# Reordering seven products and two copies in an attention and expert kernel

## The chip, the cores and the metric

The kernel runs on one core of a Trainium2 chip. The metric is the device time of one execution in microseconds (us); the time of a kernel is the median of several runs. "The profiled execution" is one further run, recorded by the hardware profiler; all rows below are from it.

## The reference

Block-sparse attention (4 batches, 8 heads, 768 tokens, head size 64) feeds a layer of four experts, all in float32:

```python
def _moe_ref(x, domain_probs, w1, w2):          # x: 3072 x 512
    p = domain_probs / (domain_probs.sum(-1, keepdims=True) + 1e-09)
    out = np.zeros((N, D), dtype=np.float32)
    for e in range(E):                           # E = 4
        h = np.maximum(x @ w1[e], 0.0)           # 512 -> 1024
        out += p[:, e:e + 1] * (h @ w2[e])       # 1024 -> 512
    return out
```

Every token passes through all four experts; `x` is the attention output, 768 tokens a batch.

## The kernel before

**Work.** The 4 x 1024 hidden features are cut into 8 chunks of 512. In batches two to four (`b` = 1 to 3 in the code) each chunk has a first layer (`first7`, 512 inputs to 512 features) and a second layer (`second7`, back to 512 outputs). Both use a seven-product scheme of Strassen's kind, with the products numbered 1 to 7: one product is six matmuls of 128x128 weights by 384 tokens (two parts of the inner dimension, three combinations of high and low halves of the float32 numbers). In the first layer a chunk has two halves, `s` = 0 and 1, of seven products each, so 14 in all; the second layer has 14 as well (`SEQ`: seven products by two parts `d`). Chunk 0 of a batch is an exception: its first layer is done plainly (`FIRST7`), as 16 products, because the operands of the scheme are only being made then.

**Accumulators.** The first layer's products 1, 6, 7 and 4 are added up in one PSUM tile, `w`, one after another: W = P1, then P1+P6, then +P7, then +P4. After each but the last the running sum is read out by another engine, and the next of them may write only when that read is done. Products 2, 5 and 3 go to a tile `v`, of which there are two buffers; the second layer uses `v` too, and tiles `u0`, `u1` of its own. There is one buffer of `w`, so product 1 of the next half has to wait until the last reader of the half before it is through.

**Evacuation.** The 384-token results of a half are combined in tiles `ha` (named by `block(g, half)` in the code). `finish` (L889) takes ReLU and multiplies by the expert's weight of each token: one VectorE instruction, which reads either PSUM (`ha<-v,pb`, `ha<-w,pb`) or, for the two blocks that were already combined in SBUF, SBUF (`ha<-ha,pb`). The other sums are VectorE additions (L912, L916, L919, L922), and two copies are on ScalarE (L910, L914).

**From first to second layer.** `hidden` makes the second layer's operands from the finished `ha` tiles: sums and differences, and for each operand a ScalarE cast to the high half (L934) and a GpSimd subtraction for the low half (L935). Each second-layer product is added by VectorE to the running outputs `tot` (L1021), once or twice; product 5 goes to two outputs. In chunk 0 the first of these are ScalarE copies (L1019).

**What sets the order.** All engines run the program's order; there is no reordering scheduler. `experts` writes it: it emits first-layer and second-layer products alternately, the second layer of one chunk beside the first layer of the next, so that a second-layer product stands between two first-layer ones, except for two places in each batch, since chunk 0 has two more products. While batches two and three are in this stage, attention work of the next batch is put in between at given times (`drive`). Weights come by DMA in the products' order (`operands`, L674), and the conversion of the next batch's inputs is tied to positions in the list of products. The last chunk of the last batch has its own order (`SEQ_END`, `STEPS_END`) and ends with four stores of 384 KB.

Of the kernel before, what the change touches and what calls it, by code (L numbers as in the profile page):

```python
# [17 lines left out]
P = 128  # L18
# [5 lines left out]
def attention_moe_kernel(ctx: ExitStack, tc, qb, kb, vr, sampled, sampled_t, probs, w1, w2, out):  # L24
# [556 lines left out]
    def convert(b, limit=PLAIN):  # L581
        if b in pieces and steps.get(b, 0) < limit:
# [4 lines left out]
    L = len(ORDER)  # L587

    FIRST = [((0, 0, 0), 0), ((0, 1, 0), 0), ((1, 0, 0), 0), ((0, 0, 1), 2), ((0, 1, 1), 2),
             ((1, 1, 0), 0), ((1, 0, 1), 2), ((1, 1, 1), 2)]  # L590
# [49 lines left out]
    def operands():  # L640
# [29 lines left out]
        for b in range(1, B):  # L670
            for c in range(NCH):
                for s, n in ORDER if c else PLAIN8:
                    o = wp.tile([P, 2, KH, P], F32R, name="wo", bufs=NWO)
                    nc.sync.dma_start(f32(o), kept1[c, s, n])  # L674
                    wo[b, c, s, n] = o
                    yield
# [201 lines left out]
    def first7(b, c, s, n):  # L878
# [26 lines left out]
        else:  # L905
            if n == 1:
                W[s] = ps_m.tile([P, HS], F32, name="w", bufs=1)
            product(W[s], w, x, n == 1)
        if n == 2:
            nc.scalar.copy(block(0, 0), v)  # L910
        elif n == 1:
            nc.vector.tensor_add(block(0, 0), W[s], block(0, 0))  # L912
        elif n == 5:
            nc.scalar.copy(block(1, 1), v)  # L914
        elif n == 6:
            nc.vector.tensor_add(block(1, 0), W[s], block(1, 1))  # L916
            finish(0, 0, block(0, 0))
        elif n == 3:
            nc.vector.tensor_add(v, v, block(1, 0))  # L919
            finish(0, 1, v)  # L920
        elif n == 7:
            nc.vector.tensor_add(block(1, 1), W[s], block(1, 1))  # L922
        else:
            finish(1, 0, W[s])
            finish(1, 1, block(1, 1))
        next(weights, None)
# [3 lines left out]
    def hidden(b, c):  # L930
# [13 lines left out]
        if last_one(b, c):  # L944
# [11 lines left out]
            two(6, a11)  # L956
            nc.vector.tensor_sub(a12, a12, a11)
            yield
# [34 lines left out]
    def second7(b, c, i):  # L993
# [20 lines left out]
        for g, dh in (TO_END if last else TO)[n]:  # L1014
# [5 lines left out]
            else:  # L1020
                nc.vector.tensor_add(t, ps, t)  # L1021
            if c == NCH - 1 and (LAST_END if last else LAST)[g, dh] == n and d:
                nc.sync.dma_start(bass.AP(out.tensor, out.offset + b * S * DM + dh * (DM // 2) * S + g * HS,
                                          [[S, P], [P * S, 2], [1, HS]]), tot.pop((g, dh)))
        if d:
# [9 lines left out]
    def experts():  # L1035
# [48 lines left out]
        for b in range(1, B):  # L1084
            for c in range(NCH):
                one += ([(b, c, s, n) for s, n in ORDER] if c else
                        [(b, 0, s, (half, k, g)) for s, half, g in FIRST7 for k in range(2)])
# [272 lines left out]
```

## Time and profile before

| | |
|---|---|
| median of 3 runs | 1231.64 us (1229.37 to 1233.04) |
| profiled execution | 1228.22 us, span 1226.4 us |
| TensorE matmul busy | 1188.4 us (97%) |
| VectorE busy | 809.3 us (66%) |
| GpSimd busy | 838.6 us (68%) |
| ScalarE busy | 520.6 us (42%) |
| first layer, batches two to four, chunks 1 to 7 | 42 halves of seven products |
| steady chunk of batch four | 29.1 us, 28 products |

A row of the timeline gives the start and the length in us, the engine, the line, the operation, output and inputs, their shapes, how many instructions are merged, and in brackets how long the engine had been idle and what it waited for. A row of waits gives who waited for whom, the total in us, how often, and the longest. PE is TensorE, PEld its weight loads, DVE VectorE, ACT ScalarE, POOL GpSimd, SPq the DMA queue of SyncE. A TensorE row of six matmuls lasts 1.20 us from the first start to the modelled end, but the next product starts 1.04 us after it.

### The profile page before, as it was taken

Reading aid. Unit: us, or ns where it says so; the run is one execution under the profiler, and the core shown is the slowest. Engines: PE = TensorE matmul, PEld = TensorE weight load, DVE = VectorE, ACT = ScalarE, POOL = GpSimd, SP = SyncE. Lnnn points to the kernel's source line nnn. Section 1 sums busy time; section 2 is a strip of 40 time slices with the busy share of each in tenths; the row PEclk is TensorE's granted clock in tenths of the full one; section 3 lists DMA queues with packets and bytes.
Section 4 is the critical chain, followed back from the end, with each engine's and each line's share of the span. In section 5 each row is a group of like instructions: output and inputs, shape, how many; then the busy total and the mean of one; then the engine's idle time right before and its main releaser. Section 6 shows DMA issues by size and latency. Waiting matters only on the chain.

```text
span 1226.4 us, 32022 instructions
## 1 busy us (share of the span) xinstructions
PE 1188.4 (97%) x12243; PEld 1094.1 (89%) x12243; DVE 809.3 (66%) x1701; ACT 520.6 (42%) x1259; POOL 838.6 (68%) x824
## 2 busy tenths in 40 slices
PE   7789999999999999999999999999999999999997
PEld 4578888888888988989989998999999999999997
DVE  6675766566654767667666766766566676666667
ACT  4754565656552344445433243444533332222221
POOL 7737978888776675677647875766755776666662
PEclk9989999999999999999999999999999999999999
DMA  9986879999879887889969687889876688777774
GB/s 271 253 279 239 302 254 353 298 317 328 291 264 345 285 244 228 270 269 274 277 205 346 218 270 230 281 272 277 281 243 212 221 271 270 248 263 256 256 236 154
DMA packets 206804, 326.48 MB, mean 266 GB/s; under 512 B 17483, under 2 KB 108204, under 8 KB 206652
## 3 DMA queue, kind: packets, MB, share of 16 engines
q1 hardware_dynamic: 200208, 303.53, 75.9%
q0 software_dynamic: 6400, 20.91, 5.7%
q8 instruction: 97, 1.59, 0.6%
q14 instruction: 55, 0.45, 0.1%
q10 hardware_dynamic: 44, 0.00, 0.0%
HBM read 256.69 MB, written 67.68 MB: 264 GB/s over the span
## 4 chain that ended last, share of the span: by engine, by line
PE 76%; DVE 4%; DMA 3%; issue 2%; POOL 1%; ACT 1%; SPq 0%; DVEq 0%; ACTq 0%; POOLq 0%
PE w L770 18%; PE u L1011 15%; PE v L770 14%; PE v L1011 12%; PE po L848 7%; PE o L403 3%; PE tp L390 2%; PE s L369 2%; PE s L362 1%; DMA kept<-w2o 1%; DMA w2o<-kept 1%; PE x L422 1%; DMA v<-in_vr_dram 1%; PE sw L440 1%; DVE tot L1021 1%
## 5 line engine op out<-in xcount | busy, mean ns | idle before, releaser
L935 POOL TENSOR_TENSOR ho<-ha,ho 128x768 fp32r<-128x768 f32 x165 | 318.7, 1941 | 244.1 <-ACT ho L934 241.2
L770 PE MATMUL w<-xo,wo 128*128 128x384 f32 x1524 | 308.9, 339 | 6.8 <-DVE ha L922 3.2
L770 PEld LDWEIGHTS w<-xo,wo 128*128 128x128 f32 x1524 | 267.6, 188 | 14.7 <-DVE ha L922 3.9
L934 ACT CAST ho<-ha 128x768 fp32r<-128x768 f32 x168 | 139.3, 837 | 270.0 <-DVE ha L889 106.0
L770 PE MATMUL v<-xo,wo 128*128 128x384 f32 x1176 | 239.6, 340 | 2.4 <-DMA wo<-kept 1.1
L1011 PE MATMUL u<-ho,w2o 128*128 128x384 f32 x1128 | 228.2, 338 | 2.3 <-issue 2.3
L770 PEld LDWEIGHTS v<-xo,wo 128*128 128x128 f32 x1176 | 207.4, 189 | 7.9 <-DMA wo<-kept 1.4
L1011 PEld LDWEIGHTS u<-ho,w2o 128*128 128x128 f32 x1128 | 196.9, 188 | 4.7 <-issue 2.9
L1011 PE MATMUL v<-ho,w2o 128*128 128x384 f32 x888 | 179.6, 339 | 2.8 <-issue 1.5
L1011 PEld LDWEIGHTS v<-ho,w2o 128*128 128x128 f32 x888 | 154.7, 188 | 6.5 <-DVE ha L889 2.7
L1021 DVE TENSOR_TENSOR tot<-v,tot 128x384 f32<-128x384 f32 x184 | 97.9, 552 | 91.3 <-PE v L1011 89.9
L1021 DVE TENSOR_TENSOR tot<-u,tot 128x384 f32<-128x384 f32 x180 | 98.8, 552 | 47.2 <-PE u L1011 47.1
L848 PE MATMUL po<-w2o,hh 128*128 128x512 f32 x384 | 123.5, 403 | 1.9 <-DVE oacc L863 1.9
L381 ACT ACTIVATE p<-p,mx 128x256 f32<-128x256 f32 (+1 forms) x192 | 95.3, 498 | 52.4 <-DVE mx L379 52.3
L220 POOL DMA_INDIRECT v<-in_vr_dram,vidx x81 | 79.8, 985 | 23.7 <-issue 17.2
L660 POOL TENSOR_TENSOR wo<-r,wo 128x256 fp32r<-128x256 f32 x92 | 72.5, 793 | 32.2 <-ACT wo L659 31.6
L379 DVE CUSTOM_DVE_ANT_1 p<-s,mask 128x256 f32<-128x256 f32 (+1 forms) x192 | 69.7, 418 | 21.3 <-PE s L369 16.8
L889 DVE SCALAR_TENSOR_TENSOR ha<-ha,pb 128x384 f32<-128x384 f32 x84 | 83.1, 989 | 0.0
L848 PEld LDWEIGHTS po<-w2o,hh 128*128 128x128 f32 x384 | 69.0, 188 | 12.6 <-DVE oacc L863 2.7
L848 PE MATMUL po<-w2o,hl 128*128 128x512 f32 x192 | 75.8, 395 | 0.0
L403 PEld LDWEIGHTS o<-v,pt 128*32 128x32 f32 x2816 | 46.4, 110 | 21.6 <-issue 17.7
L403 PE MATMUL o<-v,pt 128*32 128x64 f32 x2816 | 55.2, 221 | 7.7 <-issue 7.0
(169 smaller groups left out, 1628.2 us busy)
## 6 DMA issues: line engine op xcount, KB each, us to landing
w2o<-kept SPq DMA_DIRECT2D x168, 512.0 KB, 4.7
wo<-kept SPq DMA_DIRECT2D x318, 256.0 KB, 4.1
kept<-wo SPq DMA_DIRECT2D x106, 256.0 KB, 5.0
v<-in_vr_dram SPq DMA_DIRECT2D x88, 192.0 KB, 6.3
kept<-w2o SPq DMA_DIRECT2D x32, 512.0 KB, 5.4
r<-in_w_dram SPq DMA_DIRECT2D x16, 512.0 KB, 5.5
r<-in_w_dram SPq DMA_DIRECT2D x32, 256.0 KB, 5.4
kept<-t SPq DMA_DIRECT2D x32, 256.0 KB, 5.9
```

The lines of the kernel that those rows point to most:

```text
L220: nc.gpsimd.indirect_dma_start(out=v[:rows, i, 1 - i], out_offset=None, in_=vr, element_offset=b * S * DM, in_offset=bass.IndirectOffsetOn ...
L379: nc.vector.tensor_tensor_reduce(p.rearrange("p (a b) -> p a b", b=BLOCK), s[h][:n, i], mk, -SCALE, 3.0e38, ALU.add, ALU.min, mx[:n])
L381: nc.scalar.activation(p, p, AF.Exp, bias=mx[:n], scale=-1.0, accum_out=self.sums[:n, m:m + 1])
L403: nc.tensor.matmul(o[cs, m], self.pt[:, 2 * m + k, cs], vs[c][:, k, e], start=k == 0, stop=k == 1)
L660: nc.gpsimd.tensor_sub(o[:, 1], src, f32(o[:, 0]))
L770: nc.tensor.matmul(ps, w[:, wi, t], x[:, xi, t], start=fresh and m == 0, stop=m == 3 * KH - 1, skip_group_check=not fresh)
L848: nc.tensor.matmul(p, a[:, js], w[:, i], start=f == 0 and n == 0, stop=f == FT - 1 and n == 2)
L889: nc.vector.scalar_tensor_tensor(block(g, half), src, 0.0, q, op0=ALU.max, op1=ALU.mult)
L934: nc.scalar.copy(o[:, 0], src)
L935: eng.tensor_sub(o[:, 1], src, f32(o[:, 0]))
L1011: nc.tensor.matmul(ps, w[:, j, wi, ds], h[:, hi, j], start=fresh and m == 0, stop=m == 5, skip_group_check=not fresh)
L1021: nc.vector.tensor_add(t, ps, t)
```

## The change

In chunks 1 to 7 of batches two to four the first layer's products come in the order 1 2 6 5 7 3 4 in place of 2 1 5 6 3 7 4. The sums are formed another way: ScalarE copies W after product 1 and after product 6, and `v` after product 5; VectorE adds `v` of products 2 and 5 to them, and W of product 7 to the copy of 5. The finish of block (1, 1), which followed product 4, now follows product 3. In the last chunk the difference a12 - a11 is computed on GpSimd instead of VectorE, and the last output block is stored in two DMAs of 192 KB, each as soon as its part is done, instead of one of 384 KB.

```diff
@@ -586,6 +586,9 @@
     ORDER = [(s, n) for s in range(2) for n in (2, 1, 5, 6, 3, 7, 4)]
     L = len(ORDER)
+    ORDER7 = [(s, n) for s in range(2) for n in (1, 2, 6, 5, 7, 3, 4)]
@@ -669,7 +672,7 @@
-                for s, n in ORDER if c else PLAIN8:
+                for s, n in ORDER7 if c else PLAIN8:
                     o = wp.tile([P, 2, KH, P], F32R, name="wo", bufs=NWO)
                     nc.sync.dma_start(f32(o), kept1[c, s, n])
@@ -906,23 +909,24 @@
             product(W[s], w, x, n == 1)
-        if n == 2:
-            nc.scalar.copy(block(0, 0), v)
-        elif n == 1:
-            nc.vector.tensor_add(block(0, 0), W[s], block(0, 0))
+        if n == 1:
+            nc.scalar.copy(block(0, 0), W[s])
+        elif n == 2:
+            nc.vector.tensor_add(block(0, 0), v, block(0, 0))
+        elif n == 6:
+            nc.scalar.copy(block(1, 0), W[s])
+            finish(0, 0, block(0, 0))
         elif n == 5:
             nc.scalar.copy(block(1, 1), v)
-        elif n == 6:
-            nc.vector.tensor_add(block(1, 0), W[s], block(1, 1))
-            finish(0, 0, block(0, 0))
+            nc.vector.tensor_add(block(1, 0), v, block(1, 0))
+        elif n == 7:
+            nc.vector.tensor_add(block(1, 1), W[s], block(1, 1))
         elif n == 3:
             nc.vector.tensor_add(v, v, block(1, 0))
             finish(0, 1, v)
-        elif n == 7:
-            nc.vector.tensor_add(block(1, 1), W[s], block(1, 1))
+            finish(1, 1, block(1, 1))
         else:
             finish(1, 0, W[s])
-            finish(1, 1, block(1, 1))
         next(weights, None)
@@ -954,7 +958,7 @@
             two(6, a11)
-            nc.vector.tensor_sub(a12, a12, a11)
+            nc.gpsimd.tensor_sub(a12, a12, a11)
@@ -1019,9 +1023,12 @@
-            if c == NCH - 1 and (LAST_END if last else LAST)[g, dh] == n and d:
-                nc.sync.dma_start(bass.AP(out.tensor, out.offset + b * S * DM + dh * (DM // 2) * S + g * HS,
-                                          [[S, P], [P * S, 2], [1, HS]]), tot.pop((g, dh)))
+            if c == NCH - 1 and (LAST_END if last else LAST)[g, dh] == n:
+                at0 = out.offset + b * S * DM + dh * (DM // 2) * S + g * HS
+                if last and n == 3:
+                    nc.sync.dma_start(bass.AP(out.tensor, at0 + d * P * S, [[S, P], [1, HS]]), t)
+                elif d:
+                    nc.sync.dma_start(bass.AP(out.tensor, at0, [[S, P], [P * S, 2], [1, HS]]), tot.pop((g, dh)))
@@ -1083,7 +1090,7 @@
-                one += ([(b, c, s, n) for s, n in ORDER] if c else
+                one += ([(b, c, s, n) for s, n in ORDER7] if c else
```

Three places show what it does to the engines' order. The first is TensorE in a steady chunk of batch four, from product 7 or 3 of half 0 to the first products of half 1. L770 (now L773) is a first-layer product, whose number follows `xo`; L1011 (now L1015) is a second-layer product. Before:

```order
L770 MATMUL v_15508<-xo3_14220,wo_15367 128x384 x6
L1011 MATMUL v_15519<-ho_15410,w2o_15377 128x384 x6
L770 MATMUL w_15447<-xo7_14557,wo_15386 128x384 x6
L1011 MATMUL v_15541<-ho_15414,w2o_15395 128x384 x6
L770 MATMUL w_15447<-xo4_14462,wo_15405 128x384 x6
L1011 MATMUL u0_15458<-ho_15444,w2o_15442 128x384 x6
L770 MATMUL v_15567<-xo2_14112,wo_15433 128x384 x6
L1011 MATMUL v_15578<-ho_15414,w2o_15395 128x384 x6
L770 MATMUL w_15592<-xo1_14137,wo_15455 128x384 x6
```

And now:

```order
L773 MATMUL w_15458<-xo7_14585,wo_15399 128x384 x6
L1015 MATMUL v_15552<-ho_15444,w2o_15409 128x384 x6
L773 MATMUL v_15565<-xo3_14248,wo_15421 128x384 x6
L1015 MATMUL v_15577<-ho_15448,w2o_15430 128x384 x6
L773 MATMUL w_15458<-xo4_14490,wo_15439 128x384 x6
L1015 MATMUL u0_15492<-ho_15478,w2o_15476 128x384 x6
L773 MATMUL w_15602<-xo1_14164,wo_15467 128x384 x6
L1015 MATMUL v_15613<-ho_15448,w2o_15430 128x384 x6
```

Between 7 and 4, which share a `w`, there were one product and there are now three; between 4 and the next half's product 1, which uses the same buffer, there were three and there is now one.

The second place is VectorE over the same products: additions (L919, L922; now L925, L923), finishes (L889, now L892) and the second layer's additions to `tot` (L1021, now L1025). Before:

```order
L919 TENSOR_TENSOR v_15508<-v_15508,ha_15473 128x384
L889 SCALAR_TENSOR_TENSOR ha_15473<-v_15508,pb_14820 128x384
L1021 TENSOR_TENSOR tot_14581<-v_15519,tot_14581 128x384
L922 TENSOR_TENSOR ha_15473<-w_15447,ha_15473 128x384
L1021 TENSOR_TENSOR tot_14665<-v_15541,tot_14665 128x384
L1021 TENSOR_TENSOR tot_14667<-v_15541,tot_14667 128x384
L889 SCALAR_TENSOR_TENSOR ha_15431<-w_15447,pb_14820 128x384
L889 SCALAR_TENSOR_TENSOR ha_15473<-ha_15473,pb_14820 128x384
```

And now:

```order
L923 TENSOR_TENSOR ha_15506<-w_15458,ha_15506 128x384
L1025 TENSOR_TENSOR tot_14609<-v_15552,tot_14609 128x384
L925 TENSOR_TENSOR v_15565<-v_15565,ha_15506 128x384
L892 SCALAR_TENSOR_TENSOR ha_15506<-v_15565,pb_14850 128x384
L892 SCALAR_TENSOR_TENSOR ha_15506<-ha_15506,pb_14850 128x384
L1025 TENSOR_TENSOR tot_14695<-v_15577,tot_14695 128x384
L1025 TENSOR_TENSOR tot_14697<-v_15577,tot_14697 128x384
L892 SCALAR_TENSOR_TENSOR ha_15465<-w_15458,pb_14850 128x384
```

The finish that reads SBUF only (`ha<-ha`) stood behind the one that releases `w` (`ha<-w`); it now stands ahead of it, with the two additions to `tot`.

The third place is TensorE where a batch goes from chunk 0 to chunk 1, the last two products of chunk 0 and the first of chunk 1. Before:

```order
L770 MATMUL w_14510<-xo7_14198,wo_14217 128x384 x6
L1011 MATMUL u1_14301<-ho_14394,w2o_14392 128x384 x6
L770 MATMUL w_14510<-xo3_14220,wo_14361 128x384 x6
L770 MATMUL v_14546<-xo2_14112,wo_14378 128x384 x6
L770 MATMUL w_14562<-xo1_14137,wo_14404 128x384 x6
```

And now:

```order
L773 MATMUL w_14538<-xo7_14227,wo_14245 128x384 x6
L1015 MATMUL u1_14329<-ho_14422,w2o_14420 128x384 x6
L773 MATMUL w_14538<-xo3_14248,wo_14389 128x384 x6
L773 MATMUL w_14574<-xo1_14164,wo_14406 128x384 x6
L773 MATMUL v_14590<-xo2_14139,wo_14432 128x384 x6
```

Product 1, which writes `w`, now follows the last product of chunk 0, which writes `w` as well, with nothing between them.

## The prediction

> **What bounds the kernel now.** I read the page first, then TensorE's waits, then the stretches, then the timeline of one steady chunk.
>
> ```profile
> PE 1188.4 (97%) x12243; PEld 1094.1 (89%) x12243; DVE 809.3 (66%) x1701; ACT 520.6 (42%) x1259; POOL 838.6 (68%) x824
> PEclk9989999999999999999999999999999999999999
> PE 76%; DVE 4%; DMA 3%; issue 2%; POOL 1%; ACT 1%; SPq 0%; DVEq 0%; ACTq 0%; POOLq 0%
> ```
>
> TensorE is the bound, at a granted clock of 0.8 in one slice of forty and 0.9 or more in the others. The change removes no product, so it can only shorten or lengthen the time in which TensorE stands still. In batch four there is none of that to take:
>
> ```profile
> 1000.00:1200.00 200.00, 200.00 (x1156) 199.98 (x1155) 132.66 (x219) 55.44 (x86) 132.06 (x70) 1.00 0.77 252
> ```
>
> Matmul busy is 200.00 of 200.00 us (second number). The waits on the results that the change rearranges all lie before that, in batches two and three:
>
> ```profile
> PE w L770 <- DVE ha L922: 3.2, 2, 1.6
> PE w L770 <- DVE ha L912: 1.3, 1, 1.3
> PE v L1011 <- DVE ha L889: 0.9, 2, 0.6
> ```
>
> These three, 5.4 us, are all that a better order can win here. The first is product 4 held by the addition that reads W after product 7, which is the tightest spot of the old order.
>
> **The change part by part.** Four accumulating products share one `w`. The new order moves the tight spot from 7→4 to 4→next 1. Whether that costs anything is read from a steady chunk of batch four; in this stretch the first-layer products of half 0 are 3, 7, 4 and then product 2 of half 1:
>
> ```profile
> 1095.05 0.57 DVE L919 TENSOR_TENSOR v<-v,ha 128x384 f32<-128x384 f32 x1 [0.29 <-PE v L770]
> 1095.65 0.56 DVE L889 SCALAR_TENSOR_TENSOR ha<-v,pb 128x384 f32<-128x384 f32 x1
> 1095.89 1.20 PE L770 MATMUL w<-xo,wo 128*128 128x384 f32 x6
> 1096.93 1.20 PE L1011 MATMUL v<-ho,w2o 128*128 128x384 f32 x6
> 1096.95 3.65 POOL L935 TENSOR_TENSOR ho<-ha,ho 128x768 fp32r<-128x768 f32 x2 [0.94 <-ACT ho L934]
> 1097.13 0.56 DVE L922 TENSOR_TENSOR ha<-w,ha 128x384 f32<-128x384 f32 x1 [0.46 <-PE w L770]
> 1097.97 1.20 PE L770 MATMUL w<-xo,wo 128*128 128x384 f32 x6
> 1098.17 1.02 DVE L1021 TENSOR_TENSOR tot<-v,tot 128x384 f32<-128x384 f32 x2 [0.48 <-PE v L1011]
> 1099.21 0.56 DVE L889 SCALAR_TENSOR_TENSOR ha<-w,pb 128x384 f32<-128x384 f32 x1
> 1099.69 1.33 DVE L889 SCALAR_TENSOR_TENSOR ha<-ha,pb 128x384 f32<-128x384 f32 x1
> 1100.05 1.20 PE L770 MATMUL v<-xo,wo 128*128 128x384 f32 x6
> 1100.95 0.54 DVE L1021 TENSOR_TENSOR tot<-u,tot 128x384 f32<-128x384 f32 x1
> ```
>
> A product's result can be read 1.24 us after its start (1095.89 to 1097.13). A dependent VectorE instruction follows 0.60 us after the one ahead of it (1095.05, 1095.65), an independent one 0.48 (1099.21, 1099.69). The last row of `finish` that reads only SBUF took 1.33 in place of the 0.56 of its PSUM sisters: GpSimd ran until 1096.95 + 3.65 = 1100.60, and it ended 0.42 after that.
>
> Now the new order in the same slots. Product 3 takes the slot of 1095.89, product 4 that of 1097.97, and product 1 of half 1 wants to start at 1100.05 into the same `w`. VectorE: addition for 3 at 1097.13, its finish at 1097.73, the SBUF finish at 1098.21. GpSimd is between its two subtractions at 1096.95 + 1.83 = 1098.78, so the SBUF finish ends at 1099.20. Behind it stand the two additions of the second layer's product 5 (1.02 together, begun 0.07 before the end ahead of them): until 1100.15. Only then the finish that releases `w`, 1100.07 to 1100.63, and 0.06 for TensorE to see it (a row of the tail, below): product 1 starts at 1100.69, **0.64 us late**. Ends of the range: with GpSimd out of the way the SBUF finish ends at 1098.76, the chain at 1100.19, 0.20 late; if VectorE misses the gap between the two GpSimd instructions and waits until 1100.60, it ends at 1102.45, 2.46 late. That it can miss it is shown here:
>
> ```profile
> 532.92 1.85 POOL L935 TENSOR_TENSOR ho<-ha,ho 128x768 fp32r<-128x768 f32 x1
> 534.17 2.80 DVE L889 SCALAR_TENSOR_TENSOR ha<-ha,pb 128x384 f32<-128x384 f32 x1
> 534.72 1.83 POOL L971 TENSOR_TENSOR ha<-ha 128x768 f32<-128x768 f32 x1
> ```
>
> The finish waited through two GpSimd instructions, 2.80 us. The Trainium skill (SBUF — State Buffer, section "SBUF: two separate sides") says that a VectorE instruction with two SBUF inputs and a GpSimd one exclude each other for the whole instruction, and "the other fully blocks". The 1.33 and 2.80 agree; the page does not say who gets the ports between two GpSimd instructions. If by that rule the loser always waited out the one begun, a handover would cost 0.64, and 2.46 where GpSimd's next counts as begun.
>
> There are 21 handovers from half 0 to half 1. In batch four six are like this one: 6 x 0.64 = 3.8. In chunk 1 the additions of product 5 are ScalarE copies, so 1.02 us of the chain fall away and nothing is late. In batches two and three five more have no attention work near: 5 x 0.64 = 3.2. In eight, attention matmuls stand between 3 and the next 1; they give TensorE time but put VectorE work into the same queue, so between 0 and 0.64, of which I take 0.3: 2.4. **Together +9.4** (2.2 to some 30).
>
> From a chunk's half 1 to the next chunk one addition stands in the queue, and GpSimd is idle there in the steady chunk (6.64 us ahead of 1086.23 in a row below): one addition of 0.47 less than in the case of 0.20 is below zero, nothing late.
>
> From chunk 0 to chunk 1 product 1 follows a product into `w` directly:
>
> ```profile
> 998.13 1.20 PE L770 MATMUL w<-xo,wo 128*128 128x384 f32 x6
> 999.17 1.20 PE L770 MATMUL v<-xo,wo 128*128 128x384 f32 x6
> 999.37 0.56 DVE L889 SCALAR_TENSOR_TENSOR ha<-w,pb 128x384 f32<-128x384 f32 x1 [0.48 <-PE w L770]
> ```
>
> `w` is free at 999.93 + 0.06 and product 1 wants 999.17: 0.8 late, in each of three batches: **+2.4**. Nothing excuses this one; VectorE was free there.
>
> Removed: the 5.4 us of waits above, since 4 now has two more products between it and 7, 6 waits for a ScalarE copy, and product 3's `v` is no longer wanted by the next but one. I take all, **-5.4** (0 if VectorE's lateness, which came from rows like 534.17, only moves on to the next spot).
>
> ScalarE gets 42 more copies:
>
> ```profile
> L914 ACT COPY ha<-v 128x384 f32<-128x384 f32 x42 | 20.1, 480 | 43.1 <-PE v L770 42.8
> L910 ACT COPY ha<-v 128x384 f32<-128x384 f32 x42 | 20.1, 479 | 56.6 <-PE v L770 56.6
> ```
>
> 42 x 0.48 = 20 us on an engine at 42%. It mostly stood waiting for the product when such a copy came (42.8 and 56.6 us idle). The product that needs `w` back comes 4.16 us after the start of the one copied, that is 2.9 after its result, so a copy may be 2.4 late. Taken as 0, hidden by the two products between; where the cover is gone (a cast waiting for GpSimd ahead of it) it costs what it is late, 0 to +2 in all. The weight loads only change order with the products; nothing on SP's queue moves past another kind.
>
> The last chunk:
>
> ```profile
> 1208.98 0.55 DVE L1021 TENSOR_TENSOR tot<-v,tot 128x384 f32<-128x384 f32 x1
> 1209.22 1.83 POOL L935 TENSOR_TENSOR ho<-ha,ho 128x768 fp32r<-128x768 f32 x1 [1.67 <-ACT ho L934]
> 1209.45 2.42 DVE L957 TENSOR_TENSOR ha<-ha 128x768 f32<-128x768 f32 x1
> 1209.59 1.31 PE L1011 MATMUL v<-ho,w2o 128*128 128x384 f32 x6 [0.35 <-DVE tot L1021]
> 1212.43 4.59 PE L1011 MATMUL v<-ho,w2o 128*128 128x384 f32 x24 [1.54 <-issue]
> 1215.71 0.99 PEld L1011 LDWEIGHTS v<-ho,w2o 128*128 128x128 f32 x6 [0.22 <-DVE tot L1021]
> ```
>
> The difference L957 sat on VectorE for 2.42 us, held by GpSimd, with additions behind it that product (2,0) needed: 1.54 us idle. (1208.98 + 0.55 to 1209.59 is the 0.06 used above.) Moved to GpSimd it runs behind the subtraction, 1211.05 to 1212.88; the cast (0.84) ends at 1213.74, and its VectorE subtraction at 1214.7, with product (2,1)'s addition behind that, until 1215.2. So (2,0) no longer stands, but the second part of product 5, which needs that `v`, starts at 1215.25 in place of 1215.71. **-0.5** (-1.8 to +0.2). The stores:
>
> ```profile
> 1220.54 0.39 SPq L1023 DMA_DIRECT2D out_dram<-tot  x1
> 1221.01 1.30 SPq L1023 DMA_DIRECT2D out_dram<-tot  x2
> GB/s 0 0 219 372 378 378 166 0 0 0 0 0 0 0 0 0 0 0 0 0 6 349 337 372 378 355 343 372 378 372 372 378 378 148 0 0 0 0 0 0
> ```
>
> The last row covers 1216 to 1226.4 in slices of 0.26 us: the last three stores move at a steady 340 to 378 GB/s from 1221.4 to 1224.7. The same bytes in smaller pieces end at the same time: 0, hidden by the two stores ahead; without them half a store, 197 KB at 372 GB/s, 0.5 us. The Trainium skill (DMA: Bandwidth & Descriptors, "Anatomy of one DMA") gives about 2.0 us a transfer beside its bytes; an estimate from that page is a gain of 0.45 for the shorter last one, and no run here shows it.
>
> **Sum.** 9.4 + 2.4 - 5.4 - 0.5 = +5.9 us on the profiled execution's 1228.2, so 1234.1. The runs' median, 1231.64, lies 3.4 above that execution; on it the forecast is **1237.5**, own range 1233 to 1242.
>
> **Rivals.** *GpSimd is out of the way.* This ends on the other side. What sets GpSimd's times in a chunk is this start:
>
> ```profile
> 1085.13 0.55 DVE L889 SCALAR_TENSOR_TENSOR ha<-ha,pb 128x384 f32<-128x384 f32 x1
> 1085.24 0.84 ACT L934 CAST ho<-ha 128x768 fp32r<-128x768 f32 x1 [7.64 <-DVE ha L889]
> 1085.78 0.96 DVE L963 TENSOR_TENSOR ha<-ha 128x768 f32<-128x768 f32 x1
> 1086.23 2.22 POOL L935 TENSOR_TENSOR ho<-ha,ho 128x768 fp32r<-128x768 f32 x1 [6.64 <-ACT ho L934]
> ```
>
> GpSimd's first subtraction took 2.22 in place of 1.83, beside L963, which came after the SBUF finish. That finish is now earlier, L963 comes 0.5 sooner, and GpSimd's whole chain may run 0.4 to 0.5 ahead. Its gap then falls at 1098.3, just after the SBUF finish is ready (1098.21), and a handover costs 0.20. With that everywhere and nothing under attention: 11 x 0.2 + 2.4 - 5.4 - 0.5 = -1.3, or 1230.3, not slower. It decides where the gap comes within 0.1 us of 1098.21; against it speaks that this is so narrow, and that batches two and three have other phases.
>
> *VectorE misses the gap.* The same early chain, but 0.1 us earlier still: GpSimd has begun its next when the finish is ready, and it costs 2.0 to 2.46. In batch four, where all chunks are alike, 6 x 2.3 in place of 3.8: +10, 1247.5. For it: 534.17. Against: most such rows end 0.4 behind the first GpSimd end.
>
> *ScalarE becomes the bound of `w`.* Copies that wait behind casts that wait for GpSimd hold `w` (in-order queue). At 2 us each for two or three of 84: +5, 1242. Against: the idle of 42.8 and 56.6 us ahead of these copies.
>
> **Chances.** Forecast 0.47, GpSimd out of the way 0.28, gap missed 0.13, ScalarE 0.07, a gain beyond -1.3 (waits I did not price vanish) 0.05. About 0.3%, 3.7 us, is what a measurement can tell from no change: below 1228 faster, above 1235.3 slower. The -1.3 case is within; of the forecast's 0.47 about 0.1 falls below 1235.3. So faster 0.08, same 0.35, slower 0.57. The range 1229 to 1247 leaves out a little at each end.
>
> **What would show it.** In the changed profile: waits of TensorE's `w` for L892, about 0.6 us each and some 20 of them, at the first product of half 1; three of 0.8 at chunk 1; fewer than 200.00 us busy in batch four; no wait on L923; (2,0) in the tail without its 1.54. Wrong would be: no wait on L892 in batch four (the first rival), waits of 2 us there (the second), or waits on L913 or L917 (the third).

## The result

The changed kernel takes 1239.24 us (median of 7 runs, 1236.55 to 1243.37), the kernel before, timed beside it, 1231.18 us (1227.38 to 1233.64). The ratio is 1.0069, 95% interval 1.0052 to 1.0087: **slower by 8.5 us**, 6.4 to 10.7. The forecast was 1237.5 us.

The profiled execution takes 1237.99 us, its span is 1236.3 us, 9.9 more than before. From the page of the changed kernel, the busy times and the chain of work that ended last, by engine:

```profile
PE 1195.0 (97%) x12243; PEld 1095.3 (89%) x12243; DVE 802.3 (65%) x1700; ACT 541.7 (44%) x1301; POOL 844.7 (68%) x825
...
PE 72%; DVE 9%; DMA 3%; issue 2%; ACT 1%; POOL 0%; POOLq 0%; SPq 0%; DVEq 0%; ACTq 0%
```

Its stretch in batch four (length, then busy time and instructions of TensorE, weight loads, VectorE, ScalarE and GpSimd, then clock, DMA share, GB/s):

```profile
1000.00:1200.00 200.00, 198.98 (x1138) 196.74 (x1137) 126.62 (x213) 60.52 (x96) 132.56 (x69) 1.00 0.79 257
```

TensorE does the same 12243 matmuls. VectorE's share of the chain went from 4% to 9%, though VectorE is busy for 7 us less: it works less, but more of its work is waited for. In batch four TensorE, 200.00 us of 200.00 before, stands for 1.02 us (by the rows, which overlap; the starts below say more).

Where TensorE stands is read from batches two to four, from their first first-layer product to their last: 394.0 to 1199.9 before, 393.97 to 1210.5 after. I call this **the stretch** from here on; it is 805.88 us before and 816.54 after, so it holds all of the loss. The waits of the weight loads in it, since the load is the first instruction of a product (such a wait is 0.32 us longer than the idle time of the matmul behind it, since the row of the product ahead runs on; measured by the starts below, a place costs nearly the whole of it: 0.34 us where the load waits 0.38). Columns: waiting, waited for, us in total, times, longest; "issue" is a wait for nothing that the profile shows. Before:

```profile
PEld w L770 <- DVE ha L922: 3.9, 2, 1.9
PEld u L1011 <- issue: 2.9, 3, 1.1
PEld v L1011 <- DVE ha L889: 2.7, 5, 1.0
...
PEld w L770 <- DVE ha L912: 1.6, 1, 1.6
...
PEld v L770 <- ACT ha L914: 0.7, 1, 0.7
PEld w L770 <- issue: 0.7, 1, 0.7
```

And after:

```profile
PEld w L773 <- DVE ha L892: 13.2, 17, 1.7
...
PEld w L773 <- issue: 2.5, 2, 1.8
PEld u L1015 <- issue: 2.4, 2, 1.7
...
PEld v L1015 <- DVE tot L1025: 1.7, 3, 0.7
...
PEld v L773 <- DVE ha L915: 1.2, 1, 1.2
PEld w L773 <- ACT ha L917: 1.1, 1, 1.1
...
PEld v L1015 <- issue: 0.9, 2, 0.5
...
PEld w L773 <- DVE tot L1025: 0.6, 1, 0.6
PEld v L1015 <- DVE ha L923: 0.6, 1, 0.6
```

The first row is new: product 1 of the next half, held by the finish that reads W. The four old waits on VectorE and ScalarE (3.9 + 2.7 + 1.6 + 0.7 = 8.9 us) are gone, five others are there in their place (1.7 + 1.2 + 1.1 + 0.6 + 0.6 = 5.2), and the products' rows on "issue" went from 3.6 to 5.8. These are not all of one kind. Those of before stand at the start of a product, and the two longest, of 1.1 us, are waits for VectorE that the profile doesn't name: the product starts 0.07 us behind the end of the addition to `tot` that reads a `u` (678.72 to 678.79, and 969.87 to 969.94). After the change these two are gone, two of 0.5 at the start of a product have the same mark (699.06 to 699.13, 994.00 to 994.07), and two new ones, of 1.7 and 1.8 us, stand in the middle of a product; the last section returns to them.

A second ledger gives each place its share. Every product has the start of its last matmul in both traces, so that a wait inside a product counts where it stands; what the difference between the two starts grows by from one product to the next is what that place costs. Over the stretch it grows by 10.65 us:

| place | us, measured | in the forecast |
|---|---|---|
| half 0 to half 1, batch two (chunks 2, 3, 4, 5, 7) and three (2, 3, 6, 7); the other three about 0 | +8.3: 0.86, 0.64, 0.31, 1.63, 1.50; 1.02, 0.60, 0.26, 1.51 | 5.6 |
| half 0 to half 1, batch four (chunks 2 to 7) | +2.1: 0.34, 0.34, 0.34, 0.33, 0.34, 0.37 | 3.8 |
| chunk 0 to chunk 1, three batches | +2.8: 0.92, 0.92, 0.92 | 2.4 |
| all else (old waits gone, other waits and stalls new) | -2.5 | -5.4 |

(Chunks 2 to 7 of batches two and three have twelve of these places. The prediction counted thirteen, 0.3 us too many.)

Behind the stretch come the last products (20.09 us before, 19.43 after) and the end behind the start of the last product (6.38 and 6.31).

Two pieces of the timeline of the changed kernel show why one handover costs 0.34 and another 1.51. The columns are start, length, engine, line, operation, and in brackets the idle time ahead. In a steady chunk of batch four:

```profile
1046.82 3.96 POOL L939 TENSOR_TENSOR ho<-ha,ho 128x768 fp32r<-128x768 f32 x2 [0.94 <-ACT ho L938]
...
1047.39 0.57 DVE L925 TENSOR_TENSOR v<-v,ha 128x384 f32<-128x384 f32 x1 [0.48 <-PE v L773]
1047.99 0.56 DVE L892 SCALAR_TENSOR_TENSOR ha<-v,pb 128x384 f32<-128x384 f32 x1
...
1048.47 0.62 DVE L892 SCALAR_TENSOR_TENSOR ha<-ha,pb 128x384 f32<-128x384 f32 x1
1049.01 1.01 DVE L1025 TENSOR_TENSOR tot<-v,tot 128x384 f32<-128x384 f32 x2
...
1049.94 0.54 DVE L892 SCALAR_TENSOR_TENSOR ha<-w,pb 128x384 f32<-128x384 f32 x1
...
1050.53 0.65 PEld L773 LDWEIGHTS w<-xo,wo 128*128 128x128 f32 x4 [0.38 <-DVE ha L892]
```

In batch three, chunk 7:

```profile
953.82 3.66 POOL L939 TENSOR_TENSOR ho<-ha,ho 128x768 fp32r<-128x768 f32 x2 [0.95 <-ACT ho L938]
...
955.02 0.57 DVE L925 TENSOR_TENSOR v<-v,ha 128x384 f32<-128x384 f32 x1 [0.48 <-PE v L773]
955.62 0.56 DVE L892 SCALAR_TENSOR_TENSOR ha<-v,pb 128x384 f32<-128x384 f32 x1
...
956.10 1.80 DVE L892 SCALAR_TENSOR_TENSOR ha<-ha,pb 128x384 f32<-128x384 f32 x1
...
957.82 1.01 DVE L1025 TENSOR_TENSOR tot<-v,tot 128x384 f32<-128x384 f32 x2
958.75 0.54 DVE L892 SCALAR_TENSOR_TENSOR ha<-w,pb 128x384 f32<-128x384 f32 x1
...
959.35 0.45 PE L773 MATMUL w<-xo,wo 128*128 128x384 f32 x1 [1.24 <-DVE ha L892]
```

The VectorE instructions and their order are the same. In batch four GpSimd starts 0.57 us ahead of the addition for product 3 (L925), in batch three 1.20 us ahead. So in batch four the gap between its two subtractions falls just where the SBUF finish (`ha<-ha`) is ready, and that takes 0.62 us; in batch three the gap is past, and the finish waits out the second subtraction: 953.82 + 3.66 = 957.48, and it ends 0.42 behind that, at 957.90. The 1.2 us between 0.62 and 1.80 go straight into the finish that releases `w`.

### The profile page after: what moved, and what is told of

It is laid out like the page before. It is cut to its first block, busy times and chain, and to the rows that moved or that the text cites. A ratio compares the mean times of both kernels' runs of the same rounds, so it can differ in the third digit from the quotient of the medians.

```text
span 1236.3 us, 32042 instructions
## 1 busy us (share of the span) xinstructions
PE 1195.0 (97%) x12243; PEld 1095.3 (89%) x12243; DVE 802.3 (65%) x1700; ACT 541.7 (44%) x1301; POOL 844.7 (68%) x825
## 4 chain that ended last, share of the span: by engine, by line
PE 72%; DVE 9%; DMA 3%; issue 2%; ACT 1%; POOL 0%; POOLq 0%; SPq 0%; DVEq 0%; ACTq 0%
PE w L773 18%; PE v L773 14%; PE u L1015 14%; PE v L1015 10%; PE po L851 7%; DVE ha L892 3%; PE o L403 3%; PE tp L390 2%; PE s L369 2%; DMA wo<-kept 1%; PE s L362 1%; DVE tot L1025 1%; DVE v L925 1%; PE x L422 1%; DVE p L379 1%
## 5 line engine op out<-in xcount | busy, mean ns | idle before, releaser
L773 PE MATMUL w<-xo,wo 128*128 128x384 f32 x1524 | 311.4, 340 | 12.5 <-DVE ha L892 7.9
L773 PEld LDWEIGHTS w<-xo,wo 128*128 128x128 f32 x1524 | 267.1, 189 | 25.5 <-DVE ha L892 13.2
L773 PE MATMUL v<-xo,wo 128*128 128x384 f32 x1176 | 239.1, 339 | 3.2 <-DVE xr L424 1.1
L1015 PE MATMUL u<-ho,w2o 128*128 128x384 f32 x1128 | 228.2, 338 | 2.0 <-issue 2.0
L773 PEld LDWEIGHTS v<-xo,wo 128*128 128x128 f32 x1176 | 207.2, 188 | 8.9 <-DMA wo<-kept 1.4
L1015 PEld LDWEIGHTS u<-ho,w2o 128*128 128x128 f32 x1128 | 197.1, 188 | 3.9 <-issue 3.1
L1015 PE MATMUL v<-ho,w2o 128*128 128x384 f32 x888 | 179.5, 339 | 2.6 <-DVE tot L1025 2.2
L1015 PEld LDWEIGHTS v<-ho,w2o 128*128 128x128 f32 x888 | 154.9, 188 | 6.2 <-DVE tot L1025 3.9
L1025 DVE TENSOR_TENSOR tot<-v,tot 128x384 f32<-128x384 f32 x184 | 97.9, 552 | 81.1 <-PE v L1015 77.9
L1025 DVE TENSOR_TENSOR tot<-u,tot 128x384 f32<-128x384 f32 x180 | 99.0, 553 | 49.9 <-PE u L1015 48.3
L892 DVE SCALAR_TENSOR_TENSOR ha<-ha,pb 128x384 f32<-128x384 f32 x84 | 81.8, 973 | 0.0
```

Source lines behind the costliest of these rows:

```text
L773: nc.tensor.matmul(ps, w[:, wi, t], x[:, xi, t], start=fresh and m == 0, stop=m == 3 * KH - 1, skip_group_check=not fresh)
L892: nc.vector.scalar_tensor_tensor(block(g, half), src, 0.0, q, op0=ALU.max, op1=ALU.mult)
L1015: nc.tensor.matmul(ps, w[:, j, wi, ds], h[:, hi, j], start=fresh and m == 0, stop=m == 5, skip_group_check=not fresh)
```

## Experiments

Theory A: as in the prediction, the new waits come from the SBUF finish that was moved ahead of the release of `w`, and from product 1 that follows a `w` product at chunk 1; against the prediction, the gain from the old waits is small. The rivals: the order of the products itself (one product in place of three between 4 and the next 1), GpSimd's hold alone, ScalarE's copies, or the last chunk. All ratios are to the kernel before on the same chip. Rows of waits are those of the weight loads in the stretch.

### The finish moved back

finish_back is the changed kernel with the finish of block (1, 1) behind product 4 again:

```diff
         elif n == 3:
             nc.vector.tensor_add(v, v, block(1, 0))
             finish(0, 1, v)
-            finish(1, 1, block(1, 1))
         else:
             finish(1, 0, W[s])
+            finish(1, 1, block(1, 1))
```

> The new order, with one line put back: the finish of block (1, 1), which reads only SBUF, comes again after the finish that releases w, as before. My theory is that the handover from product 4 of half 0 to product 1 of half 1 is late because this finish (0.56 us, or longer behind GpSimd) stands ahead of the release; the profile of the changed kernel has about 9.2 us late there in all. Then those waits go and about 9 us with them: a ratio to the kernel before of 0.998 to 1.002, with no wait of product 1 of half 1 left in batch four. If instead the one product between 4 and 1 is too short a cover by itself, or ScalarE's copies of W are what costs, the ratio stays at 1.005 to 1.009. If VectorE's lateness only moves to the next spot, it lies between, with new waits on the additions.

Measured: 1232.28 us, ratio 1.0009 (0.9994 to 1.0025); the stretch 810.20 us, 6.3 less than in the changed kernel. Its waits, and its windows in batch four:

```profile
PEld w L773 <- DVE ha L892: 3.3, 4, 1.0
...
PEld v L1015 <- DVE tot L1025: 2.1, 3, 0.9
...
PEld v L773 <- DVE ha L915: 1.6, 1, 1.6
```

```profile
1000.00:1200.00 200.00, 199.35 (x1150) 199.03 (x1149) 135.69 (x216) 61.83 (x100) 133.56 (x70) 1.00 0.79 257
```

The wait on L892 falls from 13.2 us in 17 times to 3.3 in 4, three of them those at chunk 1; batch four stands for 0.65 us in all, which is its chunk 1. One moved instruction makes 6.3 of the 10.7 us. I had expected about 9: by the ledger the handovers did get 8.8 us shorter, but 2.4 came back, nearly all of it (1.09 twice) at the two products that wait in the kernel before for an addition to `tot` (678.79 and 969.94 there). The one product between 4 and the next 1 is enough when the finish that reads W goes first, but for one handover (chunk 4 of batch two), which waits 1.4 us for an addition to `tot`; with that, the rival that blames the order of the products falls for this place.

### The finish left early, but not held by GpSimd

psum_finish keeps the early finish and lets it read PSUM in place of SBUF; so GpSimd can't hold it:

```diff
-            finish(1, 1, block(1, 1))
+            finish(1, 1, v)
```

> The new order, in which the finish of block (1, 1) reads v in PSUM instead of the block in SBUF, at the same place in VectorE's queue. It leaves out the right values of that block; the number of instructions is the same, and this one no longer has two SBUF inputs, so it does not wait for GpSimd. If GpSimd's hold on it is what makes the handovers of batches two and three long (1.0 to 1.5 us in several), these fall to about 0.2 to 0.3 each as in batch four: 4 to 5 us less than the changed kernel, a ratio of 1.003 to 1.004. If it is the number of instructions in the queue alone, the ratio stays at 1.006 to 1.008.

Measured: 1231.64 us, 1.0005 (0.9991 to 1.0018); the stretch 811.08 us, 5.5 less than in the changed kernel.

```profile
PEld w L773 <- DVE ha L892: 7.5, 15, 1.1
```

The wait comes nearly as often (15 for 17 times), but is short. By the ledger six handovers of batches two and three get 0.86, 0.45, 1.63, 1.23, 1.02 and 1.24 us shorter, one gets 0.74 longer, and all nine together 5.9 shorter, more than I had expected; those of batch four get 0.07 to 0.10 shorter each, 0.5 together. So the place of the finish decides that product 1 waits, and GpSimd's hold decides how long: in batches two and three 5.9 of the 8.3 us, in batch four 0.5 of 2.1.

### The chunk 0 to chunk 1 handover

parity is the changed kernel with the tiles of chunk 0's products exchanged, so that its last product goes to `v` and product 1 of chunk 1 finds `w` free. both is parity with the finish moved back.

```diff
-                W[0] = ps_m.tile([P, HS], F32, name="vw"[i % 2], bufs=2 - i % 2)
+                W[0] = ps_m.tile([P, HS], F32, name="wv"[i % 2], bufs=1 + i % 2)
```

> The new order, with the buffers of chunk 0 swapped: its odd results go to v and its even ones to w, so that the last product of chunk 0 no longer writes the w that product 1 of chunk 1 wants. My theory prices that handover at 0.8 us in each of three batches: 2.4 us less than the changed kernel, a ratio to the kernel before of about 1.005 (1.004 to 1.006), with the three waits of 0.8 gone. The rival, that the first product of chunk 0 now waits for w from product 4 of the chunk before and gives it back, leaves the ratio at 1.007.

> Both edits together, the finish put back and the buffers of chunk 0 swapped. If the two handovers are all that the new order costs, what remains is its gain: the waits of the old order that went (about 4.5 us in the profile) and 0.5 in the last chunk, so a ratio to the kernel before of 0.995 to 0.998. If the old waits come back when VectorE's order is the old one again, 1.000.

Measured: parity 1240.48 us, 1.008 (1.0058 to 1.0102); both 1234.67 us, 1.003 (1.0015 to 1.0045). Neither is faster than its kernel without the exchange. The three waits at chunk 1 are gone (-0.92 each), so their cause was right. But they come back: +1.62 at product 6 of chunk 1 in batch two, and +0.79, +0.75, +0.81 and +0.69 at second-layer products. The waits in parity that rose:

```profile
PEld v L1015 <- DVE tot L1025: 5.4, 8, 1.5
...
PEld w L773 <- ACT ha L913: 2.2, 3, 1.8
```

And the place at product 6 in its timeline:

```profile
415.09 2.56 DVE L967 TENSOR_TENSOR ha<-ha 128x768 f32<-128x768 f32 x1
...
417.68 0.83 ACT L938 CAST ho<-ha 128x768 fp32r<-128x768 f32 x1 [3.85 <-DVE ha L967]
418.42 0.47 ACT L913 COPY ha<-w 128x384 f32<-128x384 f32 x1
...
418.94 1.31 PE L773 MATMUL w<-xo,wo 128*128 128x384 f32 x6 [1.44 <-ACT ha L913]
```

This is the third rival's mechanism, in one place: the copy of W after product 1 stands on ScalarE behind a cast, the cast waited 3.85 us for a sum on VectorE, and product 6 waits 1.44 us for the copy. For both I had expected a kernel faster than before; that was wrong, because I took the 2.4 us off without asking what is late next.

chunk1 and chunk1_old have the finish moved back as well. In half 0 of chunk 1, chunk1 puts product 2 ahead of 1, with the old adding of these two; chunk1_old has that half wholly in the old order 2 1 5 6 3 7 4, with the old sums.

```diff
+    ORDER1 = [(0, 2), (0, 1)] + ORDER7[2:]          # chunk1
+    ORDER1 = ORDER[:7] + ORDER7[7:]                 # chunk1_old
...
-                for s, n in ORDER7 if c else PLAIN8:
+                for s, n in (ORDER1 if c == 1 else ORDER7) if c else PLAIN8:
...
```

> The new order with the finish put back, and in half 0 of chunk 1 product 2 ahead of product 1, added up as before the change. Product 1 then no longer follows the last product of chunk 0. With the finish put back the ratio to the kernel before was 1.0009; if the handover at chunk 1 costs 0.8 in each of three batches and hides nothing, this is 2.4 us less, a ratio of 0.998 to 1.000. If what is behind the handover (the waits for v two or three products later, for the additions to tot) takes the gain, as when the buffers of chunk 0 were swapped, it stays at 1.001 to 1.003.

> The new order with the finish put back, and half 0 of chunk 1 wholly in the old order (2 1 5 6 3 7 4, added up as before the change). With only 2 and 1 exchanged there, product 6 came right behind the addition that reads W after 1, and 0.5 to 1.4 us in each batch were given back. Here product 5 stands between, as before. If the handover at chunk 1 was worth its 0.8 us three times, the stretch of batches two to four is 2.4 us shorter than with the finish put back alone (810.2 us in its profile), and the ratio to the kernel before is 0.999 to 1.000. If the gain is given back further on, by v, the stretch stays above 809.

Measured: chunk1 1232.58 us, 1.0034 (1.0021 to 1.0047), stretch 809.55; chunk1_old 1228.97 us, 0.9985 (0.997 to 1.0001), stretch 805.75. In chunk1 the three waits go (-0.92, -0.92, -0.93), but product 6 now follows the addition of product 1 and waits for it (+1.55, +0.75, +0.75):

```profile
PEld w L774 <- DVE ha L917: 3.3, 3, 1.7
```

```profile
416.65 0.56 DVE L917 TENSOR_TENSOR ha<-w,ha 128x384 f32<-128x384 f32 x1 [1.28 <-ACT ha L915]
417.26 1.31 PE L774 MATMUL w<-xo,wo 128*128 128x384 f32 x6 [1.35 <-DVE ha L917]
```

In chunk1_old product 5 stands between 1 and 6. No row of a wait on the finish is left, and batch four is full again; the largest of the waits on VectorE and ScalarE that remain, and the windows:

```profile
PEld v L774 <- DVE ha L934: 1.6, 1, 1.6
PEld w L774 <- ACT ha L936: 1.1, 1, 1.1
...
PEld v L1034 <- DVE tot L1044: 0.9, 1, 0.9
```

```profile
1000.00:1200.00 200.00, 200.00 (x1156) 200.00 (x1155) 137.80 (x221) 60.77 (x98) 133.94 (x70) 1.00 0.79 251
```

The stretch is 2 us shorter than I had expected, and as long as that of the kernel before (805.88): the three places at chunk 1 got 0.92, 0.92 and 0.93 us shorter, and the handover in chunk 4 of batch two by 1.33. So the new order, with its two bad places mended, as it stands gains nothing over the old one. All rows of waits in the stretch add up to 35.6 us in both. In chunk1_old 10.2 of them are waits for an engine or a transfer, 25.4 are "issue"; before, 13.5 and 22.1. So the 3.3 us that the order does win are lost on "issue", and 2.8 of them are three stalls in the middle of a product (0.53, 0.49 and 1.77), of which the kernel before has none.

### Where the old waits came from

before_psum is the kernel before, with both SBUF finishes reading PSUM instead:

```diff
-            finish(0, 0, block(0, 0))
+            finish(0, 0, W[s])
...
-            finish(1, 1, block(1, 1))
+            finish(1, 1, W[s])
```

> The kernel before, in which the two finishes that read only SBUF read W in PSUM instead, at the same places in VectorE's queue. It leaves out the right values of these two blocks. It asks where the old order's waits came from, which I had counted as won by the new one. If they came from finishes held by GpSimd (one took 2.80 us, 6 us ahead of a wait of product 4), they go: TensorE's waits for L922, L912 and L889, 5.4 us in the profile before, fall below 1.5, and the ratio is 0.994 to 0.997. If they come from the attention's own work in VectorE's queue, the waits stay and the ratio is 0.998 to 1.001.

Measured: 1224.47 us, 0.9965 (0.9952 to 0.9978); the stretch 802.26 us, 3.6 less than before. Its waits, and in its timeline the place that the prediction showed with a finish of 2.80 us at 534.17:

```profile
PEld w L770 <- DVE ha L912: 1.6, 1, 1.6
PEld v L1011 <- DVE ha L889: 1.5, 2, 1.0
...
PEld w L770 <- DVE ha L922: 0.4, 2, 0.2
```

```profile
532.87 1.85 POOL L935 TENSOR_TENSOR ho<-ha,ho 128x768 fp32r<-128x768 f32 x1
...
534.10 0.55 DVE L889 SCALAR_TENSOR_TENSOR ha<-w,pb 128x384 f32<-128x384 f32 x1
```

The finish takes 0.55, and the wait of product 4 on L922 falls from 3.9 us to 0.4, with the old order of products untouched. Ahead of each of the two waits stood such a held finish (2.80 us at 534.17, 3.17 at 789.85). So that wait, the larger part of what the new order was to win, takes two things together, a finish that GpSimd holds and a product 4 that stands close behind 7. Taking away either one ends it: the new order's product 4 doesn't wait there either (1.92 and 1.89 us less by the ledger). But the held finishes are still in the changed kernel: 84 of `ha<-ha`, 973 ns in the mean, 989 before.

### The last chunk

order_only is the changed kernel without the two edits of the last chunk; tail_only is the kernel before with these two alone:

```diff
-            nc.vector.tensor_sub(a12, a12, a11)
+            nc.gpsimd.tensor_sub(a12, a12, a11)
...
-            if c == NCH - 1 and (LAST_END if last else LAST)[g, dh] == n and d:
+                if last and n == 3:
+                    nc.sync.dma_start(bass.AP(out.tensor, at0 + d * P * S, [[S, P], [1, HS]]), t)
```

> The change without its last chunk: the difference a12 - a11 on VectorE and one store of 384 KB, as before. I priced the last chunk at 0.5 us gained, so this should be 0.5 us slower than the changed kernel, a ratio to the kernel before of 1.007 to 1.008, with the 1.54 us of idle in the tail again. If the last chunk gains nothing it is 1.007, if it gains all of its 1.8 us, 1.0085.

> The kernel before with the last chunk's two edits alone (the difference on GpSimd, the last output in two stores). My sum has 0.5 us gained, a ratio of 0.9990 to 1.0005; a gain of all the idle would be 0.9985, and a loss, if the two stores cost a completion each, above 1.001. In the tail's rows the stretch from product (2,0) to the end tells it.

Measured: order_only 1239.39 us, 1.0083 (1.007 to 1.0096); tail_only 1227.38 us, 0.9985 (0.9972 to 0.9999). From the last first-layer product to the last product: 20.09 us before, 19.61 in tail_only, 19.96 in order_only, 19.43 in the changed kernel: half a microsecond each way. From the start of the last product to the end: 6.38, 6.30, 6.33 and 6.31, so the stores gave 0.0 to 0.1. In the changed kernel the wait of product (2,0) is gone (-1.79), and 1.3 us of it are given back by the second part of product 5:

```profile
1221.45 1.84 POOL L961 TENSOR_TENSOR ha<-ha 128x768 f32<-128x768 f32 x1
...
1225.67 0.62 PE L1015 MATMUL v<-ho,w2o 128*128 128x384 f32 x2 [1.21 <-DVE tot L1025]
```

By its ratio tail_only is 1.8 us faster than the kernel before, 0.1 to 3.4, and the two edits account for 0.6 of it (0.47 + 0.08). In its profiled execution the stretch starts 3.5 us earlier (390.47 for 394.01), in work that the edits don't touch. In the first 90 us the granted clock was 0.94 in the kernel before and 0.98 in tail_only, which may be a part of it; but sum_in_v, at 0.94 too, starts its stretch at 391.89, so the clock alone doesn't set it. Why the work ahead of the stretch differs by some 3 us from one execution to another stays open; it is the reason that spans are less sure here than the stretch.

### One sum taken off VectorE's SBUF work

sum_in_v (the finish moved back, and) adds products 1 and 2 in the tile `v`, so that block (0, 0) is finished from PSUM and GpSimd can't hold it. sum_in_v_c1 is the same with chunk1_old's half.

```diff
         elif n == 2:
-            nc.vector.tensor_add(block(0, 0), v, block(0, 0))
+            nc.vector.tensor_add(v, v, block(0, 0))
+            finish(0, 0, v)
         elif n == 6:
             nc.scalar.copy(block(1, 0), W[s])
-            finish(0, 0, block(0, 0))
```

> The new order with the finish put back; in addition the sum of products 1 and 2 is formed in v, in PSUM, and its finish reads v, so that this finish no longer has two SBUF inputs (the values are the same). In the old order two such finishes, held by GpSimd, cost 3.6 us in later waits of TensorE. If the 4.3 us that the new order still loses with the finish put back come from the finishes of this block held by GpSimd, the stretch falls from 810.2 to about 807 us, a ratio to the kernel before of 0.998 to 0.999. If they come from the place of the new additions in VectorE's queue and from chunk 1, it stays within 1 us of 810.

> Both: the sum of 1 and 2 in v, and half 0 of chunk 1 in the old order. If both causes hold and add up, the stretch of batches two to four is near 805 us, and with 0.5 us from the last chunk the ratio to the kernel before is 0.996 to 0.999, which would beat both kernels. If the two hide one another, it is no better than the better of them.

Measured: 1232.96 us, 1.0016 (1.0001 to 1.0032), stretch 810.69 (finish_back: 810.20); and 1231.08 us, 1.0005 (0.9987 to 1.0023), stretch 809.92. No gain, which is a miss. Half of the SBUF finishes are gone, but `v` is now held for two VectorE instructions in place of one, and one product waits for that in sum_in_v:

```profile
PEld v L773 <- DVE ha L892: 2.2, 1, 2.2
```

## Why the prediction was right, and where it wasn't

**The total and its sign** held: +5.9 forecast, +8.5 (6.4 to 10.7) measured by the ratio, +9.8 in the profiled execution (1237.99 for 1228.22). So the sum was some 3 us short. Of the signs named ahead, the 17 waits on L892 and a TensorE that stands in batch four came; a wait on L923 (0.6 us), which was to be absent, came too.

**Handover from half 0 to half 1, +9.4.** Measured 10.4, and finish_back shows the cause. But that the sum is so near is luck, two errors that partly cancel: 3.8 for 2.1 in batch four, 5.6 for 8.3 in batches two and three. Batch four was given 0.64 a handover and costs 0.33 to 0.37. There the first rival had the mechanism: GpSimd's chain runs 0.39 us ahead (it starts 0.57 ahead of the addition for product 3; before, 0.18 ahead of the addition in that slot, 1096.95 to 1097.13), and the SBUF finish takes 0.62. In batches two and three the second rival had the mechanism: the finish misses the gap and takes up to 1.80. But the product is late by 0.3 to 1.6 and not by 2.0 to 2.46, because GpSimd had started earlier still and the finish waits out only what is left of the second subtraction. One price from one steady chunk had been given to both; psum_finish shows that they differ in cause, since GpSimd's hold is worth 5.9 us in the one and 0.5 in the other.

**Chunk 0 to chunk 1, 3 x 0.8.** 0.92 each, of which 0.81 at the product's first matmul and 0.11 behind it: the step with the best price, because both its ends stood in rows. What it didn't say, and parity and chunk1 show, is that these 2.4 us are not to be had by freeing product 1: the next product in line then waits.

**The old waits, -5.4: the step that failed.** All else in the stretch came to -2.5. The prediction took the gain in full, and gave as its other end "0 if VectorE's lateness, which came from rows like 534.17, only moves on to the next spot"; the result lies between the two, and only a part of it for that reason. By the ledger the places that got shorter come to 8.8 us: 1.92 and 1.89 at the product 4 behind L922, 1.09 twice at the products that had waited unnamed for an addition to `tot`, and the rest in pieces under 0.7. So the waits went, and more of them than were counted. But 6.2 us came back, which the prediction had at nothing: 1.76 and 1.72 as the two stalls in the middle of a product, and 2.7 at products that wait for VectorE or ScalarE, in the list the waits on `tot`, L915, L917 and L923. The 2.7 fit the lateness that moves on, since 3.5 of the 3.9 us on L922 needed held finishes, which the new order doesn't take away; that each of these waits comes from it is argued and was not tried one by one. The 3.5 are not VectorE's: at these two places TensorE waits for none of its results. With -2.5 in place of -5.4 the prediction's sum would have been +8.8; with the other measured terms in place as well it is the 9.9 of the span.

**ScalarE's copies, 0.** One wait, on L917, 1.1 us, within the 0 to 2 given. The third rival stayed small here; parity shows where it would come in (2.2 us on L913).

**The last chunk, -0.5, and the stores, 0.** -0.65 in the changed kernel, -0.47 in tail_only, and -0.53 between order_only and the changed kernel; the stores 0.0 to -0.1. Both as worked out, with what product 5 gives back. The Trainium skill's page on transfers (DMA: Bandwidth & Descriptors, "Anatomy of one DMA — SWDGE (gpsimd) path") gave an estimate of 0.45 us for a shorter last store; that section is about transfers issued by GpSimd, these stores are issued by SyncE, and these runs show at most 0.08.

## What to carry to other kernels

When an in-order engine frees the buffer that the bound engine waits for, the instruction that frees it comes first, and work that a third engine can hold up comes behind it: one finish moved by one place cost 6.3 of 10.7 us. Before a new order is credited with an old wait, ask what had made the engine late there, by taking that cause away in the old order; if it is an engine's lateness, a new order can leave it there for the next buffer. And look for what the new order makes TensorE wait for besides data: a third of this loss stood where, as far as the profile shows, no engine's result was awaited. A price from one steady chunk holds for chunks with the same phase between the engines, and parts with other work beside them need a row of their own.

## What was not expected of the hardware

A VectorE instruction with two SBUF inputs gets its turn between two GpSimd instructions only if it is ready when the first ends, and the lengths of both show it. Where it got the gap (1048.47, 0.62 us) GpSimd's two subtractions took 3.96 us together; where it waited (956.10, 1.80 us) they took 3.66. So the gap costs GpSimd 0.30. To be ready is not always enough: the finish at 534.17 of the kernel before begins 0.55 us ahead of GpSimd's next (534.72) and still waited that out. In the profiles before and after, 51 such finishes began beside a GpSimd instruction with another right behind it: 48 ended 0.41 to 0.42 us behind the first, three (534.17 and 789.85 before, 461.02 after) 2.20 us behind it, so behind the second; what else decides stays open. Additions that read one tile in PSUM took their usual time beside a running GpSimd (1049.01, 1.01 us for two, as at 957.82 with GpSimd just ended). The Trainium skill (SBUF — State Buffer, "SBUF: two separate sides") describes a lock that the one that starts first keeps for its whole instruction, and names a VectorE instruction with two SBUF inputs against a GpSimd one that reads SBUF as one case of it; these lengths agree. That this lock decided 3.6 us of the kernel before, in waits that its profile puts down to an addition that was itself never held, was the surprise.

Some products stand still in their middle behind attention work, with nothing in the profile that they wait for. One of the changed kernel:

```profile
529.90 0.86 PE L1015 MATMUL u<-ho,w2o 128*128 128x384 f32 x4 [1.59 <-issue]
```

There are two of them in the changed kernel, 3.5 us together, and none before: of the thirteen profiles the three with the old order (before, tail_only, before_psum) have none over 0.25 us, the ten with the new order two or three each, 25 in all, of 0.49 to 2.29 us. They are not the wait for a tile, since the product's first matmuls have run. What the trace does show beside them is a transfer. From the page of the changed kernel (queue and kind; packets, MB, share of the time of 16 engines):

```profile
q8 instruction: 97, 1.59, 0.5%
```

These are 97 transfers of 16 KB. One of them starts 2.26 to 2.78 us ahead of the end of every one of the 25 stalls, whatever the stall's own length; for the one above it starts between 527.5 and 527.6. So these products most likely wait for TensorE's own next instructions. No run took that wait away, and why the transfer comes too late with the new order and not with the old stays open.
